# Moving the three big SBUF buffers of a KV-cache decode kernel to multiples of 4096 bytes

## The chip, the cores and the metric

The kernel runs on one core of one Trainium2 chip. The metric is the device time of one execution in microseconds (us); lower is better. "The profile" is one execution recorded by the hardware profiler; its span, from the first recorded work to the last, is 1.8 us shorter than that execution's time.

HBM is the main memory. SBUF is the core's memory, addressed by partition (128 of them) and by the byte within a partition. The DMA engines copy between the two in packets, and the profiler records each packet's start, length and duration.

## The reference, cut to what matters

Two branches on a token `x` of shape (2, 1, 1024), mixed by a gate. Branch A is attention for one new position over a cache of 16384 positions, 32 heads and batch 2; branch B is a small MLP block.

```python
q = (x @ wq) ...                                            # wq 1024 x 4096
scores = einsum("bhqd,bhkd->bhqk", q, k_cache) * Dh**-0.5   # k_cache 2 x 32 x 16384 x 128, bf16
o = einsum("bhqk,bhkd->bhqd", softmax(scores), v_cache)     # v_cache the same shape
a = o.reshape(...) @ wo
b = mlp_block(x, w1, w2, w3, w4)     # h = gelu(LN(x) @ w1) is shifted along the sequence, then @ w2
return g * a + (1 - g) * b           # g = sigmoid(sum(x * gate_w))
```

The two caches are 537 MB of the 572.5 MB that the kernel reads. Each byte is used once.

## The kernel before

Everything large goes through three SBUF buffers of 64 KiB per partition ("big"). 32 tiles of K and 32 of V (8 MiB each) and the weights take turns in them.

```python
    NBIG = 3
    small = ctx.enter_context(tc.tile_pool(name="small", bufs=1))
    big = ctx.enter_context(tc.tile_pool(name="big", bufs=NBIG))      # lies behind small
    const = ctx.enter_context(tc.tile_pool(name="const", bufs=1))     # lies behind big
    # ...
    def big_tile(name):
        return big.tile([P, SLOT], BF16, tag="big", name=name)        # SLOT = 32768 elements
    # ...
    def load_k(i):                                                    # load_v likewise
        t = big_tile("Kn")
        nc.sync.dma_start(out=t[:].rearrange("p (j d) -> p j d", d=Dh), in_=cache_rows(A_k_cache, i))
    # ...
    def qk_stage(i):
        # ... 16 times per tile: VectorE transposes a piece of K into one of two buffers T,
        for m in range(NM):
            T = t_tile([P, 2, CJ, 32], FP32)
            moved = nc.vector.transpose(
                out=T[:].rearrange("p w j s -> p j w s"),
                in_=Kw[:, m * CW : (m + 1) * CW].rearrange("p (j w e) -> p j w e", w=2, e=32),
            )
            # ... and TensorE multiplies it with the query:
            for v in range(4):
                nc.tensor.matmul(S[:], lhsT=z[...], rhs=Tb[...], start=..., stop=...)
```

The order per tile is: scores of K tile i+1, then the product with V tile i, then the softmax of tile i+1. In the built program each partition's share of a K or V tile is one run of 65536 bytes, and the trace has one packet for it.

## Time and profile before

| | before |
|---|---|
| time, median | 1334.7 us |
| bytes read from HBM | 572.53 MB |
| main DMA queue, share of 16 engines' span | 99.4% |
| TensorE (PE) busy, VectorE (DVE) busy | 60%, 57% |

The profile of before, its view of DMA: the busy share of the DMA engines in 40 equal slices (9 is 90% or more), the packets, and the queues with packets, MB and the share of the 16 engines' span that their packets took. q1 is the kernel's own queue; q8 fetches instructions.

```profile
DMA  9999999999999999999999999999999999999998
...
DMA packets 12377, 573.27 MB, mean 430 GB/s; under 512 B 1384, under 2 KB 1392, under 8 KB 2203
...
q1 hardware_dynamic: 12313, 572.53, 99.4%
q8 instruction: 39, 0.64, 0.2%
```

The DMA engines are full from start to end, so the time is the sum of packet times, and anything that makes packets shorter or longer must show. The engines are the other candidate. The profile of before, groups of instructions: line, engine, operation, output and input, count, then busy us and mean ns, then the idle time just before them and what ended it. Below it, from the same profile's waits of VectorE: total us, times, longest.

```profile
L388 DVE STREAM_TRANSPOSE T<-Kn 128x1024 f32<-128x1024 f32 x512 | 612.0, 1229 | 252.5 <-DMA Kn<-in_A_k_cache_dram 199.1
```

### The profile page before, as it was taken

The numbers are of one execution on the slowest core, as the hardware profiler recorded it, in microseconds if no ns is written. First come the engines' busy times: TensorE is split into PE (matmuls) and PEld (weight loads), VectorE is DVE, ScalarE is ACT, GpSimd is POOL, SyncE is SP. The second block draws the span as 40 slices with busy tenths as digits, with TensorE's granted clock in tenths as the row PEclk, the third lists the DMA queues.
The fourth block names the chain that finished last, engine by engine and source line by source line (L and its number), as shares of the span: only waits on it lengthen the run. The fifth ranks groups of instructions, "written<-read, shape, count | busy, mean of one in ns | idle before, by whom it ended". The sixth has DMA issues, their size and how long they took to land.

```text
span 1333.3 us, 11505 instructions
## 1 busy us (share of the span) xinstructions
PE 805.6 (60%) x4982; PEld 354.5 (27%) x5045; DVE 759.7 (57%) x1001; ACT 27.2 (2%) x68; POOL 12.8 (1%) x40
## 2 busy tenths in 40 slices
PE   2577655766556755556665555566655556665564
PEld 1223222332225322222222222222222222222231
DVE  1677665475652665555666555566655556666540
ACT  0000000000000000000000000000000000000000
POOL 0000000000000000000000000000000000000000
PEclk9788777787777777788887777888777788877775
DMA  9999999999999999999999999999999999999998
GB/s 410 439 437 433 423 437 431 427 434 431 439 428 441 431 423 437 441 437 425 433 437 431 433 433 437 433 431 437 435 429 433 437 437 425 435 435 433 431 421 337
DMA packets 12377, 573.27 MB, mean 430 GB/s; under 512 B 1384, under 2 KB 1392, under 8 KB 2203
## 3 DMA queue, kind: packets, MB, share of 16 engines
q1 hardware_dynamic: 12313, 572.53, 99.4%
q8 instruction: 39, 0.64, 0.2%
q14 instruction: 11, 0.09, 0.0%
q10 hardware_dynamic: 14, 0.01, 0.0%
HBM read 572.53 MB, written 0.00 MB: 429 GB/s over the span
## 4 chain that ended last, share of the span: by engine, by line
PE 31%; DVE 30%; DMA 23%; another core or an unknown queue 12%; issue 2%; ACT 1%; ACTq 0%; SPq 0%; DVEq 0%
DVE T L388 23%; PE S L402 20%; DMA Kn<-in_A_k_cache_dram 13%; PE O L446 7%; DMA wt<-in_B_w_dram 4%; DMA Vn<-in_A_v_cache_dram 3%; DMA wo<-in_A_wo_dram 3%; PE misc L255 2%; DVE Os L461 2%; ACT Pr L430 1%; DVE PT L434 1%; PE misc L604 1%; PE misc L585 1%; DVE mx L423 1%
## 5 line engine op out<-in xcount | busy, mean ns | idle before, releaser
L402 PE MATMUL S<-T,z 128*128 128x512 bf16 x1985 | 583.6, 423 | 323.7 <-DVE T L388 304.5
L388 DVE STREAM_TRANSPOSE T<-Kn 128x1024 f32<-128x1024 f32 x512 | 612.0, 1229 | 252.5 <-DMA Kn<-in_A_k_cache_dram 199.1
L402 PEld LDWEIGHTS <-z 128*128 128x128 bf16 x2048 | 211.2, 104 | 682.8 <-issue 521.5
L446 PE MATMUL O<-Vn,PT 128*32 128x512 bf16 x2048 | 121.4, 390 | 3.3 <-DMA Vn<-in_A_v_cache_dram 3.3
L446 PEld LDWEIGHTS <-PT 128*32 128x32 bf16 x2048 | 74.3, 140 | 49.2 <-issue 20.4
L457 DVE TENSOR_SCALAR Os<-O,xmask 128x128 f32<-128x128 f32 x32 | 11.2, 351 | 101.3 <-PE O L446 101.3
L255 PE MATMUL misc<-rs,ones_f 128*128 128x2 f32 x64 | 17.9, 350 | 79.1 <-DVE rs L477 79.1
L430 ACT ACTIVATE Pr<-S,nb 128x512 bf16<-128x512 f32 x32 | 22.0, 687 | 1198.9 <-DVE nb L425 1161.1
L469 PE MATMUL misc<-asel,Os 128*128 128x2 f32 x64 | 12.4, 264 | 50.9 <-DVE Os L461 50.9
L413 DVE TENSOR_REDUCE m<-S 128x1 f32<-128x512 f32 x32 | 22.1, 692 | 36.9 <-PE S L402 36.9
L434 DVE STREAM_TRANSPOSE PT<-Pr 128x512 bf16<-128x512 bf16 x32 | 22.8, 711 | 28.7 <-ACT Pr L430 28.7
L255 PEld LDWEIGHTS misc<-rs,ones_f 128*128 128x128 f32 x64 | 16.2, 314 | 83.9 <-issue 81.2
L461 DVE SCALAR_TENSOR_TENSOR Os<-O,xmask,Os 128x128 f32<-128x128 f32 x96 | 33.7, 351 | 3.4
L469 PEld LDWEIGHTS misc<-asel,Os 128*128 128x128 f32 x64 | 9.7, 192 | 65.2 <-DVE Os L461 61.0
L255 PE MATMUL misc<-mdiag,ones_f 128*128 128x128 f32 x64 | 15.5, 325 | 17.1 <-DVE mdiag L416 17.1
L423 DVE TENSOR_REDUCE mx<-misc 64x1 f32<-64x64 f32 x64 | 14.2, 222 | 19.1 <-PE misc L255 18.7
L362 POOL TENSOR_TENSOR z<-qsel,own 128x32 bf16<-128x32 bf16 x32 | 10.7, 333 | 1197.9 <-PE S L402 1168.1
L604 PE MATMUL misc<-xn2T,wt 128*128 128x2 bf16 x224 | 14.4, 202 | 8.0 <-DMA wt<-in_B_w_dram 8.0
L481 DVE RECIPROCAL rinv<-misc 128x2 f32<-128x2 f32 x32 | 5.5, 171 | 22.7 <-PE misc L255 22.7
L703 DVE CAST T<-out_acc 128x256 bf16<-128x256 f32 x1 | 0.4, 425 | 29.7 <-PE out_acc L495 29.7
L604 PEld LDWEIGHTS <-wt 128*128 128x128 bf16 x224 | 14.3, 169 | 8.2 <-DMA wt<-in_B_w_dram 8.2
L484 DVE SCALAR_TENSOR_TENSOR OT<-misc,g_bc,rinv 128x2 bf16<-128x2 f32 x32 | 7.0, 220 | 15.6 <-PE misc L469 15.6
(90 smaller groups left out, 122.3 us busy)
## 6 DMA issues: line engine op xcount, KB each, us to landing
Vn<-in_A_v_cache_dram SPq DMA_DIRECT2D x2, 4096.0 KB, 42.8
wt<-in_B_w_dram SPq DMA_DIRECT2D x1, 7168.0 KB
w<-in_B_w_dram SPq DMA_DIRECT2D x4, 1792.0 KB, 31.6
wo<-in_A_wo_dram SPq DMA_DIRECT2D x6, 1024.0 KB, 34.1
wt<-in_B_w_dram SPq DMA_DIRECT2D x1, 2048.0 KB, 37.3
wt<-in_B_w_dram SPq DMA_DIRECT2D x1, 1536.0 KB, 40.9
wo<-in_A_wo_dram SPq DMA_DIRECT2D x2, 512.0 KB, 18.8
wo<-in_A_wo_dram SPq DMA_DIRECT2D x4, 256.0 KB, 13.7
```

The source lines that it names most:

```text
L255: nc.tensor.matmul(ps[:], lhsT=ones_f[:], rhs=src, start=True, stop=True)
L388: moved = nc.vector.transpose(out=T[:].rearrange("p w j s -> p j w s"), in_=Kw[:, m * CW : (m + 1) * CW].rearrange("p (j w e) -> p j w e", ...
L402: nc.tensor.matmul(S[:], lhsT=z[:, v, NM - 1 - m : NM - 1 - m + P], rhs=Tb[:, v // 2, :, v % 2], start=(m == 0 and v == 0), stop=(m == NM ...
L413: nc.vector.reduce_max(out=m[:], in_=S[:], axis=AX.X)
L423: nc.vector.reduce_max(out=mx[pa, :], in_=mall[pa, pa], axis=AX.X)
L430: nc.scalar.activation(out=Pr[:], in_=S[:], func=ACTF.Exp, bias=nb[:], scale=scale, accum_out=rs[:])
L434: nc.vector.transpose(out=PT[:], in_=Pr[:])
L446: nc.tensor.matmul(O[32 * g : 32 * g + 32, :], lhsT=PT[:, m : CJ * 32 : 16], rhs=V[:, j0 : j0 + 4, :], start=(m == 0), stop=(m == NM - 1),)
L461: nc.vector.scalar_tensor_tensor(out=Os[:], in0=Ox, scalar=xmask[:, x : x + 1], in1=Os[:], op0=ALU.mult, op1=ALU.add,)
L469: nc.tensor.matmul(oc[:], lhsT=Os[:], rhs=asel[:], start=True, stop=True)
L585: nc.tensor.matmul(ps[group(g), :], lhsT=actT[rows, r, :], rhs=w[rows, r, g * HW : (g + 1) * HW], start=False, stop=(n == len(slots) - 1), ...
L604: nc.tensor.matmul(ps[:, c, :], lhsT=w[:, r, :].rearrange("k (p c) -> k p c", c=C)[:, :, c], rhs=actT[:, r, :], start=(r == 0), stop=(r == ...
```

## The change

Its intent is to let the big buffers start on a round address. Seven constants (3840 bytes per partition) move from the pool behind the buffers to the one in front of them, which pushes the buffers up by 3840 bytes.

```diff
-    ident_f = const.tile([P, P], FP32)
+    ident_f = small.tile([P, P], FP32)
-    perm = const.tile([P, P], BF16)
+    perm = small.tile([P, P], BF16)
-    ones_f = const.tile([P, P], FP32)
+    ones_f = small.tile([P, P], FP32)
-        z = const.tile([P, 4, ZW], BF16, name=f"z{n}")
+        z = small.tile([P, 4, ZW], BF16, name=f"z{n}")
-    qsel = const.tile([P, NHG, B, 4], BF16)
+    qsel = small.tile([P, NHG, B, 4], BF16)
-    OT = const.tile([P, B, H], BF16)
+    OT = small.tile([P, B, H], BF16)
-    h_rows = const.tile([P, D // 2], BF16)
+    h_rows = small.tile([P, D // 2], BF16)
```

Addresses in the built programs, in bytes within a partition:

```
             before                             after
big buffers  16640, 82176, 147712               20480, 86016, 151552
 mod 4096    256                                0
T buffers    213248, 217344 (256 mod 4096)      217088, 221184 (0 mod 4096)
```

No instruction is added, removed or reordered.

## The prediction

> **What bounds the kernel now.** The DMA engines. The profile's table of DMA queues gives the main queue 99.4% of the 16 engines' span of 1333.3 us (572.53 MB); counted packet by packet, no engine is idle between 20 and 1290 us. PE (60% busy) and DVE (57%) are not the limit: issues to landing take 37 to 52 us (table of DMA issues), where an 8 MiB transfer alone occupies the engines for 19.3 us, so transfers are released well before their turn.
>
> **How close to their limit the packets are.** The packet records have almost constant durations by size: 65536 B 2418 ns (7710 of 8192 exactly that), 32768 B 1213, 16384 B 611, 8192 B 309, 4096 B 159, 2048 B 84. A line through them is 8 ns + bytes / 27.2 GB/s; 16 engines of that slope are 435 GB/s, the fabric ceiling of the Trainium skill, "DMA: Bandwidth & Descriptors", section "Where 436 GB/s comes from" (435.2); the trace agrees. The data alone need 572.53 MB / 435.2 GB/s = 1315.6 us. Beyond it the packets took 6.6 us of fixed cost (8 ns each, over 16 engines) and 2.9 us of excess in few long ones (118 of the 64 KiB packets took over 50 ns more). The rest is the start (about 2 us), instruction fetches (2.3 us of engine time), and the end (4 to 5 us).
>
> **What the change does.** In the built programs the three buffers move from 16640, 82176 and 147712 (each 256 past a multiple of 4096) to 20480, 86016 and 151552 (multiples of 4096). No instruction is added, removed or reordered on any engine, nor a byte more moved. The two transpose buffers T also move from 256 past to a multiple of 4096.
>
> **What it can gain.** If crossing a 4096 boundary cost anything, the 64 KiB packets (16 crossings) would lie above the line through the small ones. They don't: 512 B and 65536 B have nearly the same fixed part. The same page, section "How a descriptor splits into AXI transactions", counts transactions from 256 B boundaries; the old addresses already lie on such. So the fabric share stays. The most that alignment could take is 6.6 + 2.9 = 9.5 us (0.7%), and I expect a small piece of it at most: a cycle per packet would be 0.9 us.
>
> **Critical path.** A change in packet time shows one for one in the span. A few per cent of DVE or PE time would be hidden: the transposes (16 of 1229 ns per tile, 19.7 us, against 38.6 us for a K and a V transfer) have slack, and keep their offset to each other.
>
> **Prediction.** 1334.0 us, 8 in 10 between 1331.5 and 1336.5. Faster by over 2%: 0.01; within 2%: 0.98; slower by over 2%: 0.01.
>
> **What would show it right.** The mode of the 64 KiB packets stays 2418 ns (2416 to 2419), the main queue at 99.3 to 99.5%, mean rate 429 to 431 GB/s, some 12300 packets, transposes 1.2 us. **Wrong:** a mode of 2400 or less (a per-crossing cost was there); fewer long packets and a span 3 us shorter (the excess was due to alignment); or transposes slower by tens of per cent with idle slices of DMA (conflicts at the new addresses).
>
> **What would make it wrong.** A cost of misaligned writes hidden inside the slope, so that what I read as the fabric's limit is not one; or a conflict of DMA writes with the engines' reads at the new addresses, which no record of before can show.

## More of the kernel before

A time quoted here is the median of the timed runs of one kernel, and the record lists every run compared as being in the fast of the chip's two states.

With a sequence of one position every shifted `h` is zero, so that `w2` multiplies zeros; one experiment uses that.

```profile
DVE T L388 <- DMA Kn<-in_A_k_cache_dram: 199.1, 30, 12.1
...
DVE T L388 <- PE S L402: 49.1, 81, 0.9
```

VectorE waits 199.1 us in all for K tiles that haven't landed, 199.1 / 32 = 6.2 us per tile. That is the slack of compute.

One view seems to say otherwise, the chain of work that ended last, as shares of the span by engine:

```profile
PE 31%; DVE 30%; DMA 23%; another core or an unknown queue 12%; issue 2%; ACT 1%; ACTq 0%; SPq 0%; DVEq 0%
```

It follows one path back and gives PE and DVE 61%.

## The result

| | before | after |
|---|---|---|
| time, median of 6 runs | 1334.71 us | 1334.83 us |
| range | 1334.65 to 1334.81 | 1334.60 to 1335.16 |

The ratio is 1.0001, with a 95% interval of 0.9988 to 1.0014. A ratio here is the mean time of one kernel's fast runs over that of the other's of the same rounds, so it is not quite the ratio of the quoted medians. The change did nothing that can be measured.

The profile after, the same views as of before: slices of DMA, packets, queues; then the transposes; then VectorE's waits.

```profile
DMA  9999999999999999999999999999999999999998
...
DMA packets 12377, 573.27 MB, mean 430 GB/s; under 512 B 1384, under 2 KB 1392, under 8 KB 2203
...
q1 hardware_dynamic: 12313, 572.53, 99.4%
q8 instruction: 39, 0.64, 0.2%
```

```profile
L388 DVE STREAM_TRANSPOSE T<-Kn 128x1024 f32<-128x1024 f32 x512 | 611.8, 1228 | 252.7 <-DMA Kn<-in_A_k_cache_dram 199.1
```

```profile
DVE T L388 <- DMA Kn<-in_A_k_cache_dram: 199.1, 30, 12.1
...
DVE T L388 <- PE S L402: 48.7, 78, 0.9
```

Queues, transposes and waits agree to the last digit or nearly so. This rules out one way for a change to look neutral: two effects that cancel. Neither the packets nor the transposes moved.

(TensorE shows 805.6 us busy before and 819.5 after. That is an artefact: the record of before holds 1985 of the 2048 score matmuls, that of after all 2048.)

The sharper view is the packet records themselves. The commonest duration of a packet by its size, in ns, and how many of the 64 KiB packets have exactly that:

```
bytes      2048   4096   8192   14336   32768   65536
before       84    159    309     535    1213    2418  (7710 of 8192)
after        84    159    309     535    1213    2418  (7773 of 8192)
```

### The profile page after: what moved, and what is told of

The parts are those of the page before. It is cut to its first block, busy times and chain, and to the rows that moved or that the text cites. A ratio compares the mean times of both kernels' runs of the same rounds, so it can differ in the third digit from the quotient of the medians.

```text
span 1333.4 us, 11568 instructions
## 1 busy us (share of the span) xinstructions
PE 819.5 (61%) x5045; PEld 354.6 (27%) x5045; DVE 759.5 (57%) x1001; ACT 27.3 (2%) x68; POOL 12.8 (1%) x40
## 3 DMA queue, kind: packets, MB, share of 16 engines
q1 hardware_dynamic: 12313, 572.53, 99.4%
HBM read 572.53 MB, written 0.00 MB: 429 GB/s over the span
## 4 chain that ended last, share of the span: by engine, by line
PE 33%; DVE 29%; DMA 23%; another core or an unknown queue 12%; issue 2%; ACT 1%; ACTq 0%; SPq 0%; DVEq 0%
DVE T L388 22%; PE S L402 21%; DMA Kn<-in_A_k_cache_dram 13%; PE O L446 7%; DMA wt<-in_B_w_dram 4%; DMA Vn<-in_A_v_cache_dram 3%; DMA wo<-in_A_wo_dram 3%; PE misc L255 2%; DVE Os L461 2%; ACT Pr L430 1%; DVE PT L434 1%; PE misc L604 1%; PE misc L585 1%; DVE mx L423 1%
## 5 line engine op out<-in xcount | busy, mean ns | idle before, releaser
L402 PE MATMUL S<-T,z 128*128 128x512 bf16 x2048 | 597.8, 425 | 309.5 <-DVE T L388 293.5
L388 DVE STREAM_TRANSPOSE T<-Kn 128x1024 f32<-128x1024 f32 x512 | 611.8, 1228 | 252.7 <-DMA Kn<-in_A_k_cache_dram 199.1
```

The costliest lines, as they stand in the source:

```text
L388: moved = nc.vector.transpose(out=T[:].rearrange("p w j s -> p j w s"), in_=Kw[:, m * CW : (m + 1) * CW].rearrange("p (j w e) -> p j w e", ...
L402: nc.tensor.matmul(S[:], lhsT=z[:, v, NM - 1 - m : NM - 1 - m + P], rhs=Tb[:, v // 2, :, v % 2], start=(m == 0 and v == 0), stop=(m == NM ...
```

## The experiments

That nothing happened has several explanations. Theory A: packets care about the SBUF address, but only about 256-byte boundaries, and 256 past 4096 already is one. Rival B: they don't care about the SBUF address at all. Rival C: every piece that straddles a boundary pays, and this cost is large. A separate question is whether the readings "DMA sets the time" and "compute has slack" were right.

All experiments but after64 change the kernel before. Eleven kernels ran. The expectations speak of "beats": the Trainium skill, "DMA: Bandwidth & Descriptors", section "How a descriptor splits into AXI transactions", counts the cost of a transfer in beats of 32 bytes. At the packets' 27.2 GB/s a beat is 1.2 ns (an estimate).

Every one was reported correct, also the three that read the caches from a wrong place on purpose: the comparison with the reference does not notice a cache shifted by a few elements, and for these "correct" means nothing.

The table has the packet durations of those about addresses: "64 KiB" is the median, then the range from the 10th to the 90th percentile, then the packets of exactly 2418 ns.

```
run        SBUF start       HBM start    time us     64 KiB ns              8192 B   4096 B
           mod 4096         shifted by   (median)    median, p10-p90, exact  median   median
before     256              0            1334.7      2418  2418-2418  7710   309      159
after      0                0            1334.83     2418  2418-2418  7773   309      159
p32        288              0            1338.96     2421  2419-2428   491   313      162
p128       384              0            1338.07     2420  2418-2427  2339   312      159
off4       260, 292, 324    0            1338.99     2421  2419-2428   500   313      162
after64    64               0            1338.39     2420  2418-2427   947   312      160
src128     256              128 B        1334.81     2418  2418-2418  7854   309      159
src4       256              4 B          1334.83     2418  2418-2418  7553   309      159
both128    384              128 B        1338.03     2420  2418-2427  2229   313      159
const32    256              0            1334.73     2418  2418-2418  7802   309      159
```

### p32: all big buffers 32 bytes further

```diff
+    small.tile([P, 16], BF16, name="pad")
     big = ctx.enter_context(tc.tile_pool(name="big", bufs=NBIG))
```

> All three big buffers start 32 bytes later than before: 288 past a multiple of 4096, no longer on a 256 byte boundary (still on a 32 byte one). Theory A (a packet pays for the 256 byte boundaries of its SBUF side, once per packet): one beat of 32 bytes more, so the 64 KiB packets go from 2418 to about 2419 ns and the run within 1 us of before. Rival B (the SBUF address costs nothing at all as long as it is on 32 bytes): 2418 ns, same time. Rival C (every 256 byte piece that straddles a boundary is split in two and pays again): several per cent at least, packets of 2500 ns or more and a run over 1360 us.

1338.96 us against 1334.86 of before on the same chip, ratio 1.0031 (1.0017 to 1.0044). The SBUF address does matter, so rival B fell, and rival C's several per cent fell too. Theory A had the right kind of cost but too small a size: not about 1 ns per packet, but 4.3 on average for 64 KiB (mean 2423.2 to 2427.5 ns); the commonest durations are 2421 and 2428 ns. The extra is about as large in an 8192-byte packet (mean 309.7 to 315.2 ns), and 2.9 ns in a 4096-byte one, so it is a cost per packet and not per byte.

The profile of p32, header and main queue:

```profile
span 1337.3 us, 11568 instructions
...
DMA packets 12377, 573.27 MB, mean 429 GB/s; under 512 B 1384, under 2 KB 1392, under 8 KB 2203
...
q1 hardware_dynamic: 12313, 572.53, 99.3%
```

The packets are the same in number and bytes, and the engines are as full; only the rate is lower. Summed over the records, the main queue's packets took 1328.2 us per engine, 3.1 more than before (1325.0), and the instruction fetches 0.3 more; the span grew by 4.0 (1333.3 to 1337.3). So a change in packet time shows in the span, as the prediction said; the last 0.6 us isn't accounted for.

The fetches are worth a look. They load none of the three buffers, yet the packets of q8 took 1067 ns on average here and 1059 to 1068 in all five runs off 256 bytes, against 938 to 941 in before, after, const32, src128, src4 and dve6 (no_w2 930, dve25 988). So the loss isn't confined to the packets whose address moved. Why is not shown.

### p128: 128 bytes further

The same edit with `[P, 64]`.

> The big buffers start 128 bytes past a 256 byte boundary. Theory A: four beats more per packet (4.7 ns), the 64 KiB packets at about 2423 ns, run about 3 us longer (1337 to 1338 us). Rival B: 2418 ns and the time of before. Rival C: packets of 2500 ns or more, run over 1360 us.

1338.07 us, ratio 1.0024 (1.0010 to 1.0037). The time is the one that theory A expected, but the packets don't support its arithmetic: 2339 packets still took exactly 2418 ns and nine in ten took 2427 or less (mean 2426.3), and 128 bytes cost a little less than 32, where counting beats asks for four times as much.

### off4: 4 bytes off

```diff
-        return big.tile([P, SLOT], BF16, tag="big", name=name)
+        return big.tile([P, SLOT + 16], BF16, tag="big", name=name)[:, 2 : 2 + SLOT]
```

> The big buffers start 4 bytes past a 32 byte boundary (260, 292, 324 past a multiple of 4096)[...]. Theory A: one or two beats more per packet (2419 to 2421 ns), run within 2 us of before. Rival B in its strong form (the SBUF address never matters): 2418 ns, same time. Rival C: packets several per cent longer or more. The small packets (2048 B 84 ns, 4096 B 159, 8192 B 309 before) tell a cost per packet from a cost per byte. The transposes read 4 byte elements and should stay at 1.23 us.

1338.99 us, ratio 1.0031, packets like those of p32. Here the buffers start 4, 36 and 68 bytes past a multiple of 256. A start that isn't even on 32 bytes costs no more than one that is on 32 but not on 256. The transposes took 1230 ns each, as expected.

### src128 and src4: the HBM side shifted instead

```diff
-        return cache[b, hg * G : (hg + 1) * G].rearrange("a s d -> (a s) d").rearrange(
-            "(p j) d -> p j d", p=P
+        e0 = (b * H + hg * G) * Sk * Dh + (64 if i < NT - 1 else 0)     # src4: 2
+        return cache.rearrange("b h s d -> (b h s d)")[e0 : e0 + P * SLOT].rearrange(
+            "(p j d) -> p j d", p=P, d=Dh
         )
```

> The SBUF side is as before; the HBM side of all K and V transfers but the last tile's starts 128 bytes past where it did (the result is wrong on purpose). Theory A holds for reads too: four beats more, 2423 ns, run 2.5 us longer. If only the reading side pays, this one is slower and p128 is not. Rival B for both sides: 2418 ns, same time.

> The HBM side of all K and V transfers but the last tile's starts 4 bytes past where it did, the SBUF side is as before (the result is wrong on purpose). With off4 it tells whether a start off the 32 byte beat costs on the reading side, the writing side or only where the two differ. Theory A: one beat more, about 2419 ns, within 1 us. If the shift between source and destination inside a beat is what costs, packets here are as long as in off4.

1334.81 and 1334.83 us, both ratios 1.0000, packets of 2418 ns. Theory A's expectation of 2423 ns for src128 missed. In this kernel neither shift of the read address in HBM costs anything, and the write address in SBUF does.

### both128: both sides shifted by the same 128 bytes

> p128 and src128 in one: the SBUF side and the HBM side of K and V both start 128 bytes past a 256 byte boundary (wrong result on purpose). Theory: only the SBUF address counts, so this run is as p128, 1337.5 to 1338.5 us. Rival (what counts is that the two sides differ within 256 bytes): 1334.8 us, since here they agree. Rival (both sides pay): over 1340 us, though src128 alone cost nothing.

1338.03 us, ratio 1.0024, equal to p128. The cost is not that source and destination differ within 256 bytes; it is where the destination starts.

### const32: the constants and T moved, the buffers not

```diff
     TW = 2 * CJ * 32
+    const.tile([P, 16], BF16, name="pad")
```

> The kernel before with 32 bytes of padding in the pool of constants, behind the big buffers: every constant and both T buffers move by 32 bytes as in p32, the big buffers stay at 256 past a multiple of 4096. Theory: the loss of p32 was the big buffers' packets, so this run is at 1334.8 plus or minus 0.5 us with 2418 ns packets. Rival (the moved constants and T buffers cost p32 its 4 us): 1338 to 1339 us.

1334.73 us, ratio 1.0000. In p32 the constants and T had moved too; here they move alone and nothing happens. The pad of p32 also moved the small tiles in front of the buffers, which const32 leaves alone; but off4 leaves them alone as well and is as slow as p32. So the 4 us of p32 came from the big buffers.

### after64: the changed kernel, spoiled by 64 bytes

The edit of p32 with `[P, 32]`, on the kernel after.

> The changed kernel with 64 bytes of padding in front of the big buffers, which then start 64 past a multiple of 4096. Theory now (a packet whose SBUF side starts off a 256 byte boundary costs 3 to 10 ns more, whatever its length, and 0 and 256 past 4096 are equally good): the loss of p32 and p128 comes back on the changed kernel, 1337.5 to 1339.5 us, with 64 KiB packets mostly at 2420 to 2428 ns. Rival (near a 4096 boundary it is something else that counts, so 64 past it is as good as 0): 1334.8 us and 2418 ns.

1338.39 us, ratio 1.0026 (1.0014 to 1.0039) to the kernel before. The loss comes back on the changed kernel as soon as the buffers leave 256-byte boundaries. With 0 and 256 equal and 4, 32, 64 and 128 off all slower, theory A holds in this form: when its SBUF side starts off a 256-byte boundary, a packet takes longer by an amount that doesn't grow with its bytes. The "3 to 10 ns, whatever its length" of the expectation was too strong. On average it was 3.1 to 4.4 ns for 64 KiB, 4.1 to 5.5 for 8192 bytes and 0.6 to 3.0 for 4096 over the five runs, and many packets paid nothing.

### dve25 and dve6: is there slack in compute?

```diff
-            moved = nc.vector.transpose(
+            for _ in range(2 if m % 4 == 0 else 1):          # dve6: m == 8
+                moved = nc.vector.transpose(
```

> Every fourth transpose is done twice (128 more of 1229 ns, 157 us of VectorE in all, 4.9 us per K tile). Theory: DMA sets the time and DVE has 199 us of waits for K transfers, about 6.2 us per tile, so the run stays within 1.5 us of before and those waits fall to about 45 us. Rival (the chain of waits, which gives DVE and PE 61% and DMA 23%, is what bounds): most of the 157 us shows, the run takes 1400 us or more.

1440.2 us, ratio 1.0795: my expectation was wrong by 105 us. The profile of dve25, queues and VectorE's waits:

```profile
q1 hardware_dynamic: 12313, 572.53, 93.4%
```

```profile
DVE T L389 <- PE S L403: 221.8, 199, 2.1
...
DVE T L389 <- DMA Kn<-in_A_k_cache_dram: 12.5, 1, 12.5
```

The waits for K are gone and the DMA engines now idle: compute took over as the limit. The waits of the transposes for the matmuls that read T grew from 49.1 to 221.8 us, and I hadn't counted them. The timeline of dve25 shows how; columns are start us, us, engine, line, operation, then idle before and releaser.

```profile
530.95 5.90 DVE L389 STREAM_TRANSPOSE T<-Kn 128x1024 f32<-128x1024 f32 x5 [1.16 <-PE S L403]
538.00 5.90 DVE L389 STREAM_TRANSPOSE T<-Kn 128x1024 f32<-128x1024 f32 x5 [1.16 <-PE S L403]
```

Five transposes (four and a repeat) are followed by a wait of 1.16 us. While VectorE repeats, TensorE runs dry; then VectorE finds both T buffers still in use. A repeat thus costs 1.23 + 1.16 = 2.4 us, and four of them 9.6 us per tile. The slack is 6.2 us per tile, so 3.4 us remain, and 32 tiles of that are 109 us; measured 105. This sum was made after the result, so that the fit is no proof: it says that the slack was read rightly and the load under-counted. A smaller load tests that.

> One of the 16 transposes of each K tile is done twice. In dve25 each repeat cost VectorE its own 1.23 us and a wait of about 1.16 us for the matmuls that still read the other T buffer, 9.6 us for four against about 6.2 us of slack, which gives 32 times 3.4 or 109 us (105 measured). One repeat then costs 2.4 us per tile, less than the slack: the run stays at 1334.8 plus or minus 0.7 us, and the waits of the transposes for K fall from 199 to about 125 us. Rival (compute is on the critical path throughout): 32 times 2.4, some 75 us more, or at least 32 times 1.2, 39 us.

1334.85 us, ratio 1.0003 (0.9989 to 1.0016; one of five runs took 1336.47), with 39 us of added VectorE work. The main queue and VectorE's waits in dve6:

```profile
q1 hardware_dynamic: 12313, 572.53, 99.4%
...
DVE T L389 <- DMA Kn<-in_A_k_cache_dram: 116.5, 29, 12.5
DVE T L389 <- PE S L403: 101.8, 135, 1.9
```

The waits for K fell by 83 us (199.1 to 116.5; 125 expected) and absorbed it all. So the chain's 61% for PE and DVE didn't mean that compute set the time: the path runs through compute because each transfer is released by it, but the DMA queue behind was never empty.

### no_w2: fewer bytes

The load of `w2` and its product are left out; the product is zero for one position, so the result stays right.

```diff
-        w2 = t[:, KC * D : (KC + BASE + MORE) * D].rearrange("p (r n) -> p r n", n=D)
-        nc.sync.dma_start(out=w2[:, 0:BASE, :], ...)            # and two more transfers
...
-        hs = half_rows("w2", shT, W2_ROWS)
...
-        nc.vector.tensor_tensor(out=x1[:], in0=xT[:], in1=hs_ps[:], op=ALU.add)
+        nc.vector.tensor_copy(out=x1[:], in_=xT[:])
```

> The load of w2 (2.10 MB in packets of 12288, 36864 and 2048 B) and its product, which is zero for this one position, are left out; the result must stay right. Theory: time follows the packets: 8 packets of 460 ns per engine, then one of 1.4 us, then some of 84 ns, so 4.8 to 5.6 us less, 1329.1 to 1329.9 us. Rival (something other than the transfers sets the pace): under 2 us less.

1331.79 us (1330.54 to 1332.79), ratio 0.9976 (0.9963 to 0.9988): 3.1 us less, below the expected 4.8 to 5.6 but above the rival's 2. The packets did shrink as expected, from 1325.0 to 1320.2 us per engine on average. But a run ends with its slowest engine. In before, the last 64 packets of 2048 bytes ended within 1.0 us of each other; in no_w2 they were spread over 1.8 us, which is part of what is missing. Two of the three transfers of `w2` have few partitions (12 and, by the row count, 40). The records don't name the engine of a packet, but the twelve packets of 36864 bytes ran three at a time, in four rounds of some 1.4 us, so that transfer loaded three engines. If the others lost only their eight packets of 460 ns, that is 3.7 us (an estimate), near the 3.1 measured. Against it stands that before ended evenly in spite of this load, so this cause is argued and not shown. This is the one version faster than both kernels, and it is so because it moves fewer bytes, which has nothing to do with the change; it also relies on a sequence of one position.

## Why the prediction was right

- **"What bounds the kernel now. The DMA engines."** Right. 3.1 us more of packet time gave 4 us more of time (p32), 39 us more of VectorE work gave none (dve6).
- **"16 engines of that slope are 435 GB/s, the fabric ceiling."** It rested on the Trainium skill, "DMA: Bandwidth & Descriptors", section "Where 436 GB/s comes from". The trace agrees: the durations lie on 8 ns + bytes / 27.2 GB/s, and 16 x 27.2 is 435. Alignment left that slope alone in every run.
- **"If crossing a 4096 boundary cost anything, the 64 KiB packets (16 crossings) would lie above the line through the small ones."** The conclusion was right, the argument wasn't: a cost per crossing grows with the bytes, so it would sit in the slope and not above the line, as the prediction's last paragraph half admits. Nor does the change remove the crossings: an aligned 64 KiB run still has 15. The 4096-byte packets decide it. They start 256 bytes past a multiple of 4096 before, so each crosses one boundary, and on one after, so none crosses: all 256 took 159 ns in both.
- **"The old addresses already lie on such"** (256-byte boundaries; the same page, "How a descriptor splits into AXI transactions"). This is the step that decided the case, and it was right: 0 and 256 are equal, and every start tried off 256 costs 3 to 4 us. There was luck in it: the page describes the reading side, and the prediction applied it to the writes without saying so. The page's count of beats did not carry over: it would make 128 bytes cost four times 32, and charges the reading side, whereas p128 cost less than p32 and src128 nothing.
- **"I expect a small piece of it at most."** There was no gain at all. The few long packets (118 before, 105 after, over 50 ns above the mode) aren't due to alignment either. They hold 2.5 and 2.6 us; the 2.9 of the prediction is all that lies above the line, not theirs alone.
- **"A few per cent of DVE or PE time would be hidden."** Right for 6% (dve6). But the sentence after it, 19.7 us of transposes against 38.6 us of transfers, suggests slack of nearly half. The real slack is 6.2 us per tile, and dve25, at 25%, went over it by 105 us.
- **"Transposes slower ... conflicts at the new addresses"** was named as a way to be wrong. It didn't happen: 1229 and 1228 ns.

## What to carry to other kernels

Where the DMA engines are full, list packet durations by size before touching addresses: durations on a straight line at the fabric's rate leave little to win, here at most 0.7%. Keep the destination of big transfers on 256 bytes and stop there: 4096 bought nothing, but one innocent 32-byte constant in front of the buffers costs 0.3%, and relatively more in shorter packets (in p32 8192-byte packets took 1.8% longer, 64 KiB ones 0.2%). Read the slack of an engine from its waits for the data, and when adding work count the handover waits it causes as well as its own time.

## What the Trainium skill lacked or had wrong

- "DMA: Bandwidth & Descriptors", "How a descriptor splits into AXI transactions": it charges bytes in front of a start off a 256-byte boundary as beats and describes the reading side. Here 128 bytes off on the HBM side cost nothing (2418 ns for 64 KiB, 1334.81 us). On the SBUF side of loads any start tried off 256 bytes cost 3.1 to 4.4 ns per 64 KiB packet on average, not in proportion to the offset (32 off: 1338.96 us; 128 off: 1338.07 us).
- No page that I read says that 256-byte alignment of the SBUF destination of a plain load matters for speed, nor that more of it (4096 against 256) doesn't: 1334.83 against 1334.71 us.
- "SBUF — State Buffer", "Summary: rules for kernel authors", advises some 358 GB/s for estimates of HBM to SBUF. This lone core held 429 GB/s over 1333 us; 358 would have put the kernel at 1599 us (an estimate, 572.53 MB over that rate). The rule names no number of busy cores. The skill isn't of one mind here: "DMA: Bandwidth & Descriptors", section "Where 436 GB/s comes from", gives ~358 as what binds, beside a measurement of 425 GB/s.
